# A decode attention kernel with a ring of four K/V slots in place of six, each pair finished in its own period, and wo loaded once near the end

## The chip, the cores and the metric

One NeuronCore of one Trainium2 chip runs the kernel; the other cores are idle. The metric is device microseconds (us) of one execution. Kernels are compared only within the same rounds.

Engines in the profile: PE is the matrix engine (PEld its weight loads), DVE the vector engine, ACT the scalar engine, SP the engine whose queue issues the loads.

## The reference

A block of one new token for 4 sequences: layer norm, attention over a cache, a gated feed-forward part.

```python
B, Sq, D = 4, 1, 640
Hq, Hkv, Sk, Dh, F = 32, 32, 4096, 192, 1536
q = (layernorm(x) @ wq)                      # wq: 640 x 6144
p = softmax(q k^T * Dh**-0.5)                # k_cache, v_cache: 4 x 32 x 4096 x 192, bf16
h = x + (p v) @ wo                           # wo: 6144 x 640
out = h + (silu(n @ w_gate) * (n @ w_up)) @ w_down,   n = layernorm(h)
```

K and V are 403 MB of the 424 MB that are read, and every byte is used once. There are 128 pairs of sequence and head; the kernel takes two heads at a time, so it works on 64 "pairs" of one 3.1 MB K chunk and one 3.1 MB V chunk. K62 is the K chunk of pair 62, the last but one. The chunks lie in the slots of a ring, buffers in on-chip memory that are used in turn.

## The kernel before

For pair i: DVE multiplies K by the broadcast query in two halves (`tt`), PE adds up the products with an identity matrix (`red`, 12 matmuls a half), DVE finishes the sum (`rsum`) and takes the maximum, PE and DVE carry the maximum across partitions (`max_t`, `hmax`, `max_b`), ACT forms the exponentials (`exps`), PE multiplies them with V (`pv`). Every fourth pair closes a group of two heads: `evac`, `o_t`, `o_tc`, then 12 matmuls with a piece of wo (`womm`).

The helper records all operations of an engine in program order and turns dependences into semaphores. Each engine therefore works strictly in the order in which the Python code emits.

```python
    NS, NPR = 6, 3                                   # ring slots, product buffers
    ring = [sb(f"ring{j}", [128, T, DH], BF16) for j in range(NS)]
    wosb = [sb(f"wo{j}", [128, 3, D], BF16) for j in range(2)]
    ...
    chunks = []                                      # order of the loads
    for i in range(NP - 2):
        chunks += [("K", i), ("V", i)]
    chunks += [("K", NP - 2), ("K", NP - 1), ("V", NP - 2), ("V", NP - 1)]
    ...
    def load(c):                                     # waits for the release of the chunk NS places earlier
        n = order[c]
        deps = [lambda: released[chunks[n - NS]]] if n >= NS else ([wq_used] if slot[c] >= 3 else [])
    ...
    for c in chunks:
        load(c)
        if c[0] == "V" and c[1] % B == (1 if c[1] < NP - B else B - 1):
            load_wo(c[1] // B)                       # 16 pieces; the last one behind the last V
    ...
    for i in range(NP):                              # software pipeline over three pairs
        tt(i, 0)
        if i >= 1:
            red(i - 1, 1); rsum(i - 1, 1); rmax(i - 1)
        tt(i, 1)
        ...
        if i >= 2:
            pv(i - 2)
        if i >= 1:
            max_t(i - 1); hmax(i - 1)
        red(i, 0)
        if i >= 1:
            max_b(i - 1); neg_m(i - 1); exps(i - 1)
        rsum(i, 0)
        ...
```

The feed-forward weights are loaded last, into slots of the ring that have come free.

## Time and profile before

| | before |
|---|---|
| time, median of the first 3 runs | 1001.67 us (1001.23 to 1002.71) |
| span in the profile | 1000.1 us |
| read from memory | 424.29 MB |
| load queue, share of 16 DMA engines' span | 99.2% |
| PE, DVE, ACT busy | 66%, 55%, 12% |
| mean granted PE clock | 0.831 |
| DVE waiting for K | 295.9 us |

From the page of the kernel before: the queue table (packets, MB, share of 16 engines' span), and from the slices the share of DMA (tenths) and the GB/s in 40 equal stretches of 25 us.

```profile
DMA  9999999999999999999999999999999999999996
GB/s 393 427 438 426 427 435 428 426 434 427 427 431 431 425 429 433 430 427 427 433 428 428 432 428 428 427 434 427 428 431 433 425 428 432 428 428 430 431 423 287
q1 hardware_dynamic: 21760, 424.29, 99.2%
```

The stream of loads is never interrupted: this is what bounds the kernel. The table of waits says the same from the side of compute (who waited for whom: total us, times, longest):

```profile
DVE prod L319 <- DMA ring<-in_A_k_cache_dram: 295.9, 62, 6.6
```

DVE has work for each pair only when K arrives and is idle in between. Compute is ahead of the loads.

The timeline of one pair in the middle (start, duration, engine, line, operation, count, idle time before it and who ended it):

```profile
508.83 3.36 DVE L319 TENSOR_TENSOR prod<-ring,qb 128x6144 f16<-128x6144 bf16 x1 [5.00 <-DMA ring<-in_A_k_cache_dram]
512.96 3.35 DVE L319 TENSOR_TENSOR prod<-ring,qb 128x6144 f16<-128x6144 bf16 x1
514.02 4.90 PE L97 MATMUL pb<-prod,identH 128*128 128x512 f16 x11
519.39 2.54 PE L97 MATMUL pb<-prod,identH 128*128 128x512 f16 x11
```

PE was idle before the first reduction, and its eleven matmuls took 4.90 us there; at full clock eleven take 2.54 us. The stretch-by-stretch view shows why: the granted clock was 0.50 from 512.0 to 518.5 us and 1.00 from 519.0 us.

The end of the timeline:

```profile
958.54 3.36 DVE L319 TENSOR_TENSOR prod<-ring,qb 128x6144 f16<-128x6144 bf16 x1 [4.83 <-DMA ring<-in_A_k_cache_dram]
983.89 0.83 PE L391 MATMUL pb<-ring,pbuf 128*16 128x384 bf16 x16
990.83 1.77 PE L522 MATMUL pb<-wg_sb,lnT 128*4 128x384 bf16 x20 [1.90 <-DVE lnT L266]
995.82 1.77 PE L532 MATMUL pb<-wd_sb,guT 128*4 128x160 bf16 x48 [1.62 <-DVE guT L528]
998.00 0.67 SPq L536 DMA_DIRECT2D out_dram<-outsb  x2
```

The last PV ends at 984.72 us. Then 15.4 us of serial work follow: transposes, wo, layer norm, feed-forward, output. The loads stop at about 995 us, so compute and stream end together, and neither has much to give.

### The profile page before, as it was taken

What the parts mean: (1) busy time and instruction counts of PE and PEld (TensorE: products, weight loads), DVE (VectorE), ACT (ScalarE), POOL (GpSimd) and SP (SyncE); (2) the same over time, 40 slices, a digit from 0 to 9 for tenths busy, and PEclk for the clock granted to TensorE, in tenths of its full rate; (3) what the DMA queues carried; (4) which work ended last, traced back from release to release, by engine and by line L of the source; (5) the groups of instructions that cost most, each with busy time, mean ns of one, the idle gap of its engine ahead of it and who ended that gap; (6) DMA issues with size and microseconds to landing.
All of it is one profiled execution on the core that took longest, in us unless ns stands there. A gap on an engine that the chain in (4) does not pass through costs nothing.

```text
span 1000.1 us, 9429 instructions
## 1 busy us (share of the span) xinstructions
PE 661.4 (66%) x4752; PEld 122.6 (12%) x3344; DVE 547.6 (55%) x450; ACT 122.6 (12%) x412; POOL 4.5 (0%) x19
## 2 busy tenths in 40 slices
PE   0676676676676676676677686676676666676686
PEld 0110110111110110110111110110110111110112
DVE  2546556546546546556546546546556546546562
ACT  0110111110110110111010110111011010110112
POOL 1000000000000000000000000000000000000000
PEclk9887887877887887887887877988888887987887
DMA  9999999999999999999999999999999999999996
GB/s 393 427 438 426 427 435 428 426 434 427 427 431 431 425 429 433 430 427 427 433 428 428 432 428 428 427 434 427 428 431 433 425 428 432 428 428 430 431 423 287
DMA packets 21849, 424.90 MB, mean 425 GB/s; under 512 B 2480, under 2 KB 2480, under 8 KB 4912
## 3 DMA queue, kind: packets, MB, share of 16 engines
q1 hardware_dynamic: 21760, 424.29, 99.2%
q8 instruction: 32, 0.52, 0.2%
q14 instruction: 9, 0.07, 0.0%
q10 hardware_dynamic: 48, 0.01, 0.0%
HBM read 424.29 MB, written 0.01 MB: 424 GB/s over the span
## 4 chain that ended last, share of the span: by engine, by line
DMA 65%; PE 23%; DVE 10%; SPq 1%; issue 1%; ACT 0%; ACTq 0%; DVEq 0%
DMA ring<-in_A_k_cache_dram 63%; PE pb L97 13%; DVE prod L319 8%; PE pb L391 3%; DMA xrow<-in_A_x_dram 2%; PE pb L329 2%; DVE sc L335 1%; PE pb L344 1%; PE pb L412 1%; PE pb L353 1%; SPq L304 1%; PE pb L286 1%; DVE msb L340 1%; PE pb L374 0%; PE pb L522 0%
## 5 line engine op out<-in xcount | busy, mean ns | idle before, releaser
L319 DVE TENSOR_TENSOR prod<-ring,qb 128x6144 f16<-128x6144 bf16 x128 | 429.1, 3353 | 303.6 <-DMA ring<-in_A_k_cache_dram 295.9
L97 PE MATMUL pb<-prod,identH 128*128 128x512 f16 x1408 | 434.2, 472 | 0.0
L344 PE MATMUL pb<-identF,msb 128*1 128x128 f32 x128 | 33.9, 362 | 301.7 <-DVE msb L340 301.7
L335 DVE TENSOR_REDUCE sc<-pb 128x32 f32<-128x512 f32 x128 | 88.1, 688 | 112.5 <-PE pb L97 112.5
L358 ACT ACTIVATE negM<-pb 128x2 f32<-128x2 f32 x64 | 11.0, 172 | 713.5 <-PE pb L353 713.5
L391 PE MATMUL pb<-ring,pbuf 128*16 128x384 bf16 x2048 | 94.7, 326 | 0.2 <-ACT pbuf L365 0.2
L365 ACT ACTIVATE pbuf<-sc,negM 64x64 bf16<-64x64 f32 x128 | 73.9, 577 | 3.0
L329 PE MATMUL pb<-prod,identH 128*128 128x512 f16 x128 | 61.3, 479 | 3.2 <-DVE prod L319 3.2
L353 PEld LDWEIGHTS pb<-negMc,ones_row 1*128 1x128 f32 x128 | 19.3, 189 | 280.5 <-issue 258.1
L391 PEld LDWEIGHTS pb<-ring,pbuf 128*16 128x16 bf16 x2048 | 46.4, 89 | 27.5 <-issue 0.5
L344 PEld LDWEIGHTS pb<-identF,msb 128*1 128x1 f32 x128 | 5.5, 81 | 329.0 <-DVE msb L340 329.0
L365 ACT ACTIVATION_READ_ACCUMULATOR pbuf<-sc,negM 64x1 f32 x128 | 41.8, 326 | 0.0
L380 ACT ACTIVATE qb<-pb 128x192 bf16<-128x192 f32 x64 | 21.2, 331 | 103.2 <-PE pb L374 103.2
L374 PEld LDWEIGHTS pb<-qsb,sel 4*64 4x64 bf16 x128 | 6.7, 101 | 163.2 <-issue 161.6
L353 PE MATMUL pb<-negMc,ones_row 1*128 1x2 f32 x128 | 24.8, 261 | 0.7 <-DVE negMc L348 0.7
L412 PE MATMUL pb<-r,orow 128*64 128x4 f32 x384 | 20.0, 231 | 0.6 <-ACT orow L399 0.6
L412 PEld LDWEIGHTS pb<-r,orow 128*64 128x64 f32 x384 | 18.6, 174 | 2.4 <-ACT orow L399 1.0
L374 PE MATMUL pb<-qsb,sel 4*64 4x192 bf16 x128 | 17.2, 265 | 1.0 <-ACT qsb L290 0.6
L348 DVE TENSOR_REDUCE negMc<-pb 1x2 f32<-1x128 f32 x64 | 17.4, 271 | 0.5 <-PE pb L344 0.5
L329 PEld LDWEIGHTS pb<-prod,identH 128*128 128x128 f16 x128 | 12.7, 99 | 32.7 <-issue 28.3
L256 PE MATMUL pb<-mv,quadm 128*128 128x2 f32 x4 | 1.2, 363 | 23.4 <-DVE mv L254 23.4
L340 DVE TENSOR_REDUCE msb<-sc 128x1 f32<-128x64 f32 x64 | 14.1, 220 | 2.2
(61 smaller groups left out, 76.1 us busy)
## 6 DMA issues: line engine op xcount, KB each, us to landing
ring<-in_A_k_cache_dram SPq DMA_DIRECT2D x64, 3072.0 KB, 29.8
ring<-in_A_v_cache_dram SPq DMA_DIRECT2D x63, 3072.0 KB, 22.8
wq_sb<-in_A_wq_dram SPq DMA_DIRECT2D x1, 7680.0 KB, 21.0
wo<-in_A_wo_dram SPq DMA_DIRECT2D x16, 480.0 KB, 23.5
ring<-in_A_v_cache_dram SPq DMA_DIRECT2D x2, 1536.0 KB, 19.3
wg_sb<-in_B_w_gate_dram SPq DMA_DIRECT2D x1, 1920.0 KB, 25.8
wu_sb<-in_B_w_up_dram SPq DMA_DIRECT2D x1, 1920.0 KB, 18.9
wd_sb<-in_B_w_down_dram SPq DMA_DIRECT2D x1, 960.0 KB, 20.8
```

What stands on the lines that cost most here:

```text
L97: return e.add_instruction(mybir.InstMatmult(name=e.bass.get_next_instruction_name(), engine=mybir.EngineType.PE, start_tensor_calc=start, ...
L319: tk["tt", n] = op("dve", lambda e: e.tensor_tensor(out=prod[n % NPR][:, :, :], in0=ring[slot[c]][:, h * TH:(h + 1) * TH, :], in1=qbs[i % ...
L329: tk["red", n] = op("pe", lambda e, j=j: (e.matmul if j == 0 else partial(held_matmul, e))(psR[n % 3][:, 0:TH * R], lhsT=identH[:, :], rhs ...
L335: tk["rsum", n] = op("dve", lambda e: e.tensor_reduce(sc[i % 3][:, h * TH:(h + 1) * TH], psR[n % 3][:, 0:TH * R].rearrange("q (t r) -> q t ...
L340: tk["rmax", i] = op("dve", lambda e: e.tensor_reduce(msb[i % 2][:, 0:1], sc[i % 3][:, :], AX.X, ALU.max), [g("rsum", 2 * i), g("rsum", 2 ...
L344: tk["maxT", i] = op("pe", lambda e: e.matmul(psS[0:1, 0:128], lhsT=msb[i % 2][:, 0:1], rhs=identF[:, :], start=True, stop=True), [g("rmax ...
L353: tk["maxB", i] = op("pe", lambda e: e.matmul(psS[:, 128:130], lhsT=ones_row[0:1, :], rhs=negMc[i % 2][0:1, 0:2], start=True, stop=True), ...
L365: tk["exp", i] = op("act", lambda e, hh=hh, r=r: e.activation(out=pbuf[b][r, :, 2 * b + hh], in_=sc[i % 3][r, :], func=ACTF.Exp, bias=negM ...
L374: tk["qb", i] = op("pe", lambda e, hh=hh: e.matmul(psQ[64 * hh:64 * hh + 64, 0:DH], lhsT=sel[32 * n:32 * n + B, b, :], rhs=qsb[32 * n:32 * ...
L380: tk["qbc", i] = op("act", lambda e: e.activation(out=qbs[i % 2][:, :], in_=psQ[:, 0:DH], func=ACTF.Copy, scale=QS), [g("qb", i), g("tt", ...
L391: tk["pv", i] = op("pe", lambda e, t=t, n=n: e.matmul(psO[p % 2][32 * n:32 * n + 4 * B, 0:2 * DH], lhsT=pbuf[b][:, t:t + 2, :].rearrange(" ...
L412: tk["oT", p] = op("pe", lambda e, j=j, hh=hh, k=k: e.matmul(psO[p % 2][64 * hh:64 * hh + 64, OC + B * j:OC + B * (j + 1)], lhsT=orow[p % ...
```

## The change

The intent is a simpler kernel with the same stream. The ring shrinks to four slots, which leaves room for wq in a place of its own. V1 no longer waits for the query projection, wo can lie whole in wq's place later, and each pair is finished in its own period, so one set of small buffers is enough.

```diff
-    NS, NPR = 6, 3
+    NS = 4
-    wosb = [sb(f"wo{j}", [128, 3, D], BF16) for j in range(2)]
+    wqsb = sb("wq_sb", [128, CD, H * DH], BF16)
+    wosb = nc.alloc_sbuf_tensor_at("wo_sb", [128, P, 3, D], BF16, offset=at(wqsb))
...
-        deps = [lambda: released[chunks[n - NS]]] if n >= NS else ([wq_used] if slot[c] >= 3 else [])
+        deps = [lambda: released[chunks[n - NS]]] if n >= NS else []
-        if c == ("V", NP - 1):                      # only the last V in halves
+        if c[1] == NP - 1:                          # the last K and the last V in halves
...
     for c in chunks:
+        if c == ("K", NP - 2):
+            wo_land = dma("sp", lambda e: e.dma_start(
+                wosb[:, :, :, :].rearrange("q p j n -> q p (j n)"),
+                wo[:, :].rearrange("(p q j) n -> q p (j n)", q=128, j=3)), S_wo, [wq_used])
         load(c)
-        if c[0] == "V" and c[1] % B == (1 if c[1] < NP - B else B - 1):
-            load_wo(c[1] // B)
...
     for i in range(NP):
+        p, b = i // B, i % B
+        if i == NP - 2:
+            for k in range(P - 1):
+                womm(k)
         tt(i, 0)
-        (red, rsum, max, exps of pair i-1 and pv of pair i-2 between the halves)
+        red(i, 0)
+        if i + 1 < NP:
+            q_b(i + 1)
+            q_bc(i + 1)
         tt(i, 1)
+        red(i, 1)
+        if b == 0 and p >= 1:
+            inv_l(p - 1)
+            o_tc(p - 1)
+        rsum(i, 0)
+        rsum(i, 1)
+        rmax(i)
+        max_t(i)
+        hmax(i)
+        max_b(i)
+        neg_m(i)
+        exps(i)
+        pv(i)
+        if b == B - 1:
+            evac(p)
+            l_sum(p)
+            o_t(p)
```

Cut from the diff: the query copies (16 small ones instead of 4), the selection matrix, PSUM banks and buffer counts that follow from the above, and the drain code behind the loop, which falls away.

More of the change, by code (lines that the diff above doesn't have):

```diff
@@ L126, in build_kernel @@
     J = DH // R
-    NS, NPR = 6, 3
-    OC = 2 * DH
+    NS = 4
     QS = 2.0 ** -4
@@ L143, in build_kernel @@
     ring = [sb(f"ring{j}", [128, T, DH], BF16) for j in range(NS)]
-    prod = [sb(f"prod{j}", [128, TH, DH], FP16) for j in range(NPR)]
-    wosb = [sb(f"wo{j}", [128, 3, D], BF16) for j in range(2)]
-    qsb = sb("qsb", [128, 4, 2 * DH], BF16)
+    prod = [sb(f"prod{j}", [128, TH, DH], FP16) for j in range(2)]
+    wqsb = sb("wq_sb", [128, CD, H * DH], BF16)
+    qsb = sb("qsb", [B, H * DH], BF16)
     pbuf = [sb(f"pbuf{b}", [128, T, 2 * B], BF16) for b in range(B)]
     qbs = [sb(f"qb{j}", [128, DH], BF16) for j in range(2)]
-    sel = sb("sel", [128, B, 64], BF16)
+    sel = sb("sel", [B, 2, B, 128], BF16)
     identF = sb("identF", [128, 128], FP32)
@@ L162, in build_kernel @@
     mv = sb("mv", [128, 8], FP32)
-    sc = [sb(f"sc{j}", [128, T], FP32) for j in range(3)]
+    sc = [sb(f"sc{j}", [128, T], FP32) for j in range(2)]
     msb = [sb(f"msb{j}", [128, 1], FP32) for j in range(2)]
@@ L166, in build_kernel @@
     negM = [sb(f"negM{j}", [128, 2], FP32) for j in range(2)]
-    lsb = [sb(f"lsb{j}", [128, B], FP32) for j in range(2)]
+    lsb = sb("lsb", [128, B], FP32)
     invL = sb("invL", [128, B], FP32)
-    orow = [sb(f"orow{j}", [128, 2 * DH], FP32) for j in range(2)]
-    OT = [sb(f"OT{j}", [128, 3, B], BF16) for j in range(2)]
-    sig = sb("sig", [128, FQ], FP32)
+    orow = sb("orow", [128, 2 * DH], FP32)
+    OT = sb("OT", [128, P, 3, B], BF16)
+    sig = orow
+    assert FQ == 2 * DH
     gu = sb("gu", [128, FQ], BF16)
@@ L174, in build_kernel, with at @@
     outsb = sb("outsb", [128, DQ], BF16)
-    def at(j):
-        return nc.lookup_mloc(ring[j]).addr
-    assert at(5) - at(3) == 2 * T * DH * 2
-    wqsb = nc.alloc_sbuf_tensor_at("wq_sb", [128, CD, H * DH], BF16, offset=at(3))
+    def at(t):
+        return nc.lookup_mloc(t).addr
+    assert P * 3 * D == CD * H * DH
+    wosb = nc.alloc_sbuf_tensor_at("wo_sb", [128, P, 3, D], BF16, offset=at(wqsb))
     n0 = 2 * NP
-    wgsb = nc.alloc_sbuf_tensor_at("wg_sb", [128, CD, F], BF16, offset=at(n0 % NS))
-    wusb = nc.alloc_sbuf_tensor_at("wu_sb", [128, CD, F], BF16, offset=at((n0 + 1) % NS))
-    wdsb = nc.alloc_sbuf_tensor_at("wd_sb", [128, CF, D], BF16, offset=at((n0 + 2) % NS))
+    wgsb = nc.alloc_sbuf_tensor_at("wg_sb", [128, CD, F], BF16, offset=at(ring[n0 % NS]))
+    wusb = nc.alloc_sbuf_tensor_at("wu_sb", [128, CD, F], BF16, offset=at(ring[(n0 + 1) % NS]))
+    wdsb = nc.alloc_sbuf_tensor_at("wd_sb", [128, CF, D], BF16, offset=at(ring[(n0 + 2) % NS]))
     PB = [eg.enter(nc.psum_tensor(f"pb{k}", [128, 512], FP32)) for k in range(8)]
-    psR, psS, psO, psH, psQ = PB[0:3], PB[3], PB[4:6], PB[6], PB[7]
+    psR, psS, psO, psH, psQ, psL, psT = PB[0:2], PB[2], PB[3], PB[4], PB[5], PB[6], PB[7]
     S_ring = [sem(f"s_ring{j}") for j in range(NS)]
-    S_wo = [sem(f"s_wo{j}") for j in range(2)]
-    S_x, S_out, S_half = sem("s_x"), sem("s_out"), sem("s_half")
+    S_x, S_wq, S_wo, S_out, S_halfK, S_halfV = (sem(n) for n in ("s_x", "s_wq", "s_wo", "s_out", "s_halfk", "s_halfv"))
     xd = [dma("act", lambda e, n=n: e.dma_start(xrow[32 * n:32 * n + B, :], x[:, 0, n * DQ:(n + 1) * DQ]), S_x)
           for n in range(4)]
+    wq_land = dma("sp", lambda e: e.dma_start(
+        wqsb[:, :, :].rearrange("q c n -> q (c n)"), wq[:, :].rearrange("(q c) n -> q (c n)", c=CD)), S_wq)
     chunks = []
@@ L237, in build_kernel @@
         t.deps.append(zx)
-    zp = None
-    for k in (6, 0, 1, 2, 7, 4, 5):
-        zp = op("dve", lambda e, k=k: e.memset(PB[k][:, 0:2 * DH], 0.0))
+    for ps in (psH, psO):
+        zp = op("dve", lambda e, ps=ps: e.memset(ps[:, 0:2 * DH], 0.0))
     op("dve", lambda e: e.memset(epsv[:, :], eps))
-    ksel = op("dve", lambda e: e.tensor_copy(
-        out=sel[:, :, :], in_=r32[:, 0:B][:, :, None].broadcast_to([128, B, 64])), [c1])
+    zsel = op("dve", lambda e: e.memset(sel[:, :, :, :], 0.0))
+    for hh in range(2):
+        ksel = op("dve", lambda e, hh=hh: e.tensor_copy(
+            out=sel[:, hh, :, 64 * hh:64 * hh + 64], in_=r32[0:B, 0:B][:, :, None].broadcast_to([B, B, 64])), [c1, zsel])
     kquad = op("dve", lambda e: e.tensor_scalar(
@@ L275, in build_kernel @@
                                          rhs=xrow[:, :], start=True, stop=False), [kidb, zp] + xd)
-    wq_land = dma("sp", lambda e: e.dma_start(
-        wqsb[:, :, :].rearrange("q c n -> q (c n)"), wq[:, :].rearrange("(q c) n -> q (c n)", c=CD)), S_ring[3])
-    bank = [PB[0], PB[1], PB[2], PB[7]]
+    bank = [PB[0], PB[1], psQ, psL]
     qcopy = []
@@ L288, in build_kernel @@
                     rhs=wqsb[:, c, p * 2 * DH:(p + 1) * 2 * DH], start=(c == 0), stop=(c == CD - 1)),
-                    [ln1, wq_land, zp])
-        qcopy.append(op("act", lambda e, k=k: e.activation(
-            out=qsb[:, k, :], in_=bank[k][:, 0:2 * DH], func=ACTF.Copy, scale=1.0), [a]))
+                    [ln1, wq_land])
+        for n in range(4):
+            p = 4 * k + n
+            o, i_ = qsb[:, p * 2 * DH:(p + 1) * 2 * DH], bank[k][32 * n:32 * n + B, 0:2 * DH]
+            if n % 2 == 0:
+                qcopy.append(op("act", lambda e, o=o, i_=i_: e.activation(out=o, in_=i_, func=ACTF.Copy, scale=1.0), [a]))
+            else:
+                qcopy.append(op("dve", lambda e, o=o, i_=i_: e.tensor_copy(out=o, in_=i_), [a]))
     wq_used = a
+    q_done = qcopy[-2:]
     def load(c):
         n = order[c]
-        deps = [lambda: released[chunks[n - NS]]] if n >= NS else ([wq_used] if slot[c] >= 3 else [])
+        deps = [lambda: released[chunks[n - NS]]] if n >= NS else []
         r = ring[slot[c]]
-        if c == ("V", NP - 1):
+        if c[1] == NP - 1:
             s = src(c).rearrange("q (t d) -> q t d", d=DH)
-            landed[c] = [dma("sp", lambda e, a=a, k=k: e.dma_start(r[:, a:a + TH, :], s[:, a:a + TH, :]), k, deps)
-                         for a, k in ((0, S_ring[slot[c]]), (TH, S_half))]
+            landed[c] = [dma("sp", lambda e, a=a: e.dma_start(r[:, a:a + TH, :], s[:, a:a + TH, :]), k, deps)
+                         for a, k in ((0, S_ring[slot[c]]), (TH, S_halfK if c[0] == "K" else S_halfV))]
         else:
@@ L305, in load, with half @@
                              S_ring[slot[c]], deps)]
-    wo_land = {}
-    def load_wo(p):
-        wo_land[p] = dma("sp", lambda e: e.dma_start(
-            wosb[p % 2][:, :, :].rearrange("q j n -> q (j n)"),
-            wo[p * 2 * DH:(p + 1) * 2 * DH, :].rearrange("(q j) n -> q (j n)", j=3)),
-            S_wo[p % 2], [lambda: tk["womm", p - 2]] if p >= 2 else [])
+    def half(c, h):
+        return landed[c][min(h, len(landed[c]) - 1)]
     def tt(i, h):
@@ L319, in tt @@
         tk["tt", n] = op("dve", lambda e: e.tensor_tensor(
-            out=prod[n % NPR][:, :, :], in0=ring[slot[c]][:, h * TH:(h + 1) * TH, :],
+            out=prod[h][:, :, :], in0=ring[slot[c]][:, h * TH:(h + 1) * TH, :],
             in1=qbs[i % 2][:, None, :].broadcast_to([128, TH, DH]), op=ALU.mult),
-            landed[c] + [g("qbc", i), g("red", n - NPR)])
+            [half(c, h), g("qbc", i), g("red", n - 2)])
         if h == 1:
@@ L329, in red @@
             tk["red", n] = op("pe", lambda e, j=j: (e.matmul if j == 0 else partial(held_matmul, e))(
-                psR[n % 3][:, 0:TH * R], lhsT=identH[:, :], rhs=prod[n % NPR][:, :, j * R:(j + 1) * R],
-                start=(j == 0), stop=(j == J - 1)), [g("tt", n), g("rsum", n - 3), kidh, qcopy[-1]])
+                psR[h][:, 0:TH * R], lhsT=identH[:, :], rhs=prod[h][:, :, j * R:(j + 1) * R],
+                start=(j == 0), stop=(j == J - 1)), [g("tt", n), g("rsum", n - 2), kidh] + q_done)
     def rsum(i, h):
@@ L335, in rsum @@
         tk["rsum", n] = op("dve", lambda e: e.tensor_reduce(
-            sc[i % 3][:, h * TH:(h + 1) * TH], psR[n % 3][:, 0:TH * R].rearrange("q (t r) -> q t r", r=R),
-            AX.X, ALU.add), [g("red", n), g("exp", i - 3)])
+            sc[i % 2][:, h * TH:(h + 1) * TH], psR[h][:, 0:TH * R].rearrange("q (t r) -> q t r", r=R),
+            AX.X, ALU.add), [g("red", n), g("exp", i - 2)])
     def rmax(i):
-        tk["rmax", i] = op("dve", lambda e: e.tensor_reduce(msb[i % 2][:, 0:1], sc[i % 3][:, :], AX.X, ALU.max),
+        tk["rmax", i] = op("dve", lambda e: e.tensor_reduce(msb[i % 2][:, 0:1], sc[i % 2][:, :], AX.X, ALU.max),
                            [g("rsum", 2 * i), g("rsum", 2 * i + 1), g("maxT", i - 2)])
@@ L365, in exps @@
             tk["exp", i] = op("act", lambda e, hh=hh, r=r: e.activation(
-                out=pbuf[b][r, :, 2 * b + hh], in_=sc[i % 3][r, :], func=ACTF.Exp, bias=negM[i % 2][r, hh:hh + 1],
-                scale=alpha, accum_out=lsb[p % 2][r, b:b + 1]),
-                [g("negM", i), g("rsum", 2 * i + 1), g("pv", i - B), g("lsum", p - 2), pool_done])
+                out=pbuf[b][r, :, 2 * b + hh], in_=sc[i % 2][r, :], func=ACTF.Exp, bias=negM[i % 2][r, hh:hh + 1],
+                scale=alpha, accum_out=lsb[r, b:b + 1]),
+                [g("negM", i), g("rsum", 2 * i + 1), g("pv", i - B), g("lsum", p - 1), pool_done])
     def q_b(i):
         p, b = i // B, i % B
-        k, n = p // 4, p % 4
         for hh in range(2):
             tk["qb", i] = op("pe", lambda e, hh=hh: e.matmul(
-                psQ[64 * hh:64 * hh + 64, 0:DH], lhsT=sel[32 * n:32 * n + B, b, :],
-                rhs=qsb[32 * n:32 * n + B, k, hh * DH:(hh + 1) * DH], start=True, stop=True),
-                [qcopy[k], qcopy[-1], ksel, g("qbc", i - 1), tk.get("invL")])
+                psQ[:, 0:DH], lhsT=sel[:, hh, b, :], rhs=qsb[:, (2 * p + hh) * DH:(2 * p + hh + 1) * DH],
+                start=(hh == 0), stop=(hh == 1)), q_done + [ksel, g("qbc", i - 1)])
     def q_bc(i):
@@ L381, in q_bc, with pv @@
                                                         scale=QS), [g("qb", i), g("tt", 2 * (i - 2) + 1)])
-    def pv(i, lo=0, hi=T):
+    def pv(i):
         p, b = i // B, i % B
@@ L387, in pv, with l_sum @@
         v = ring[slot[c]]
-        for t in range(lo, hi, 2):
+        for t in range(0, T, 2):
             n = (t // 2) % 4
-            land = landed[c][min(t // TH, len(landed[c]) - 1)]
             tk["pv", i] = op("pe", lambda e, t=t, n=n: e.matmul(
-                psO[p % 2][32 * n:32 * n + 4 * B, 0:2 * DH],
+                psO[32 * n:32 * n + 4 * B, 0:2 * DH],
                 lhsT=pbuf[b][:, t:t + 2, :].rearrange("q t m -> q (t m)"),
                 rhs=v[:, t:t + 2, :].rearrange("q t d -> q (t d)"),
-                start=(b == 0 and t < 8), stop=(b == B - 1 and t >= T - 8)), [land, g("exp", i), g("otc", p - 2)])
+                start=(b == 0 and t < 8), stop=(b == B - 1 and t >= T - 8)),
+                [half(c, t // TH), g("exp", i), g("evac", p - 1), zp])
         released[c] = tk["pv", i]
     def evac(p):
-        tk["evac", p] = op("act", lambda e: e.activation(out=orow[p % 2][:, :], in_=psO[p % 2][:, 0:2 * DH],
-                                                         func=ACTF.Copy), [g("pv", B * p + B - 1), g("oT", p - 2)])
-    def l_sum(p, qbc_i):
-        tk["lsum", p] = op("pe", lambda e: e.matmul(psQ[:, 256:256 + B], lhsT=halfm[:, :], rhs=lsb[p % 2][:, :],
+        tk["evac", p] = op("act", lambda e: e.activation(out=orow[:, :], in_=psO[:, 0:2 * DH], func=ACTF.Copy),
+                           [g("pv", B * p + B - 1), g("oT", p - 1)])
+    def l_sum(p):
+        tk["lsum", p] = op("pe", lambda e: e.matmul(psL[:, 0:B], lhsT=halfm[:, :], rhs=lsb[:, :],
                                                     start=True, stop=True),
-                           [g("exp", B * p + B - 1), g("qbc", qbc_i), pool_done])
+                           [g("exp", B * p + B - 1), g("invL", p - 1), pool_done] + q_done)
     def o_t(p):
@@ L412, in o_t @@
                     tk["oT", p] = op("pe", lambda e, j=j, hh=hh, k=k: e.matmul(
-                        psO[p % 2][64 * hh:64 * hh + 64, OC + B * j:OC + B * (j + 1)],
-                        lhsT=orow[p % 2][:, k * DH + j:(k + 1) * DH:3],
+                        psT[64 * hh:64 * hh + 64, B * j:B * (j + 1)],
+                        lhsT=orow[:, k * DH + j:(k + 1) * DH:3],
                         rhs=r32[:, 2 * B * k + hh:2 * B * (k + 1):2], start=(k == 0), stop=(k == 1)),
-                        [g("evac", p), pool_done])
+                        [g("evac", p), g("otc", p - 1), pool_done])
     def inv_l(p):
-        tk["invL", p] = tk["invL"] = op("dve", lambda e: e.reciprocal(invL[:, :], psQ[:, 256:256 + B]), [g("lsum", p)])
+        tk["invL", p] = op("dve", lambda e: e.reciprocal(invL[:, :], psL[:, 0:B]), [g("lsum", p)])
     def o_tc(p):
         tk["otc", p] = op("dve", lambda e: e.tensor_tensor(
-            out=OT[p % 2][:, :, :], in0=psO[p % 2][:, OC:OC + 3 * B].rearrange("q (j b) -> q j b", b=B),
+            out=OT[:, p, :, :], in0=psT[:, 0:3 * B].rearrange("q (j b) -> q j b", b=B),
             in1=invL[:, None, :].broadcast_to([128, 3, B]), op=ALU.mult),
-            [g("oT", p), g("invL", p), g("womm", p - 2)])
+            [g("oT", p), g("invL", p)])
     def womm(p):
@@ L430, in womm @@
                 tk["womm", p] = op("pe", lambda e, j=j, n=n: e.matmul(
-                    psH[32 * n:32 * n + B, 0:DQ], lhsT=OT[p % 2][:, j, :],
-                    rhs=wosb[p % 2][:, j, n * DQ:(n + 1) * DQ], start=False, stop=(p == P - 1 and j == 2)),
-                    [g("otc", p), wo_land[p]])
+                    psH[32 * n:32 * n + B, 0:DQ], lhsT=OT[:, p, j, :],
+                    rhs=wosb[:, p, j, n * DQ:(n + 1) * DQ], start=False, stop=(p == P - 1 and j == 2)),
+                    [g("otc", p), wo_land])
     for c in chunks:
+        if c == ("K", NP - 2):
+            wo_land = dma("sp", lambda e: e.dma_start(
+                wosb[:, :, :, :].rearrange("q p j n -> q p (j n)"),
+                wo[:, :].rearrange("(p q j) n -> q p (j n)", q=128, j=3)), S_wo, [wq_used])
         load(c)
-        if c[0] == "V" and c[1] % B == (1 if c[1] < NP - B else B - 1):
-            load_wo(c[1] // B)
     q_b(0)
@@ L442, in build_kernel @@
     for i in range(NP):
+        p, b = i // B, i % B
+        if i == NP - 2:
+            for k in range(P - 1):
+                womm(k)
         tt(i, 0)
-        if i >= 1:
-            red(i - 1, 1)
-            rsum(i - 1, 1)
-            rmax(i - 1)
-        tt(i, 1)
+        red(i, 0)
         if i + 1 < NP:
@@ L451, in build_kernel @@
             q_bc(i + 1)
-        if i >= 4 and (i - 4) % B == 3:
-            womm((i - 4) // B)
-        if i >= 3 and (i - 3) % B == 3:
-            p = (i - 3) // B
-            o_t(p)
-            l_sum(p, i + 1 if i + 1 < NP else i)
-        if i >= 2:
-            pv(i - 2)
-            if (i - 2) % B == 3:
-                evac((i - 2) // B)
-        if i >= 1:
-            max_t(i - 1)
-            hmax(i - 1)
-        red(i, 0)
-        if i >= 1:
-            max_b(i - 1)
-            neg_m(i - 1)
-            exps(i - 1)
-        rsum(i, 0)
-        if i >= 3 and (i - 3) % B == 3:
-            p = (i - 3) // B
-            inv_l(p)
-            o_tc(p)
-    i = NP - 1
-    red(i, 1)
-    rsum(i, 1)
-    rmax(i)
-    max_t(i)
-    hmax(i)
-    max_b(i)
-    neg_m(i)
-    exps(i)
-    load_act = op("act", lambda e: e.activation(out=mv[:, 3:4], in_=epsv[:, 0:1], func=ACTF.Sqrt))
-    if ("womm", P - 2) not in tk:
-        womm(P - 2)
-    pv(i - 1)
-    pv(i, 0, TH)
-    l_sum(P - 1, i)
+        tt(i, 1)
+        red(i, 1)
[14 more added lines that the diff above has]
+            l_sum(p)
+            o_t(p)
+    op("act", lambda e: e.activation(out=stats[:, 7:8], in_=epsv[:, 0:1], func=ACTF.Sqrt))
     inv_l(P - 1)
-    pv(i, TH, T)
-    evac(P - 1)
-    o_t(P - 1)
     o_tc(P - 1)
@@ L513, in build_kernel @@
             wd_land[c] = t
-    zg = op("dve", lambda e: e.memset(PB[0][:, 0:FQ], 0.0), [g("red", 2 * NP - 1)])
+    zg = op("dve", lambda e: e.memset(PB[0][:, 0:FQ], 0.0))
     zg = op("dve", lambda e: e.memset(PB[1][:, 0:FQ], 0.0))
```

## The prediction

> **What bounds the kernel now.** The DMA engines. The queue table says the loading queue's packets fill 99.2% of 16 engines' span, and the slices show 423 to 438 GB/s from the second slice to the last but one. 424.29 MB are read[...].  In the table of waits DVE waits 295.9 us for K to land: compute is ahead of the loads. In the timeline the last weights land at about 995.5 us (issued at 973, 22 us to landing), so one K/V pair costs the stream (estimate: 994 us x 6.29/424.29 MB) 14.7 us. The end is nearly balanced: the last PV ends at 984.7 and 15.4 us of serial work follow to 1000.1.
>
> **What the change does.** Bytes are the same: wo moves from 16 pieces to one, 7.9 MB, in front of the last two pairs. The start is the same: wq, K0, V0, K1 are issued at once in both; V1, issued at 31.2 us before, was not needed earlier. No saving on the bound.
>
> The software pipeline goes: pair i's PV now stands in front of pair i+1's reduction on PE. Costs from the timeline (us): tt 3.35 each; twelve-matmul reduction 2.75 at full clock, 5.2 at half; from the end of the second reduction to the negated maximum 1.7; from there to the end of the exponentials 1.9; PV 1.5 at full clock (about 2.6 at half, estimate). Serial period, when K is already there: 1.9+1.5 to 2.6 (tt(i+1,0) hides under it), both reductions 6.4 to 7.7 with a mixed clock, query broadcast 0.3, 1.7: 12.5 to 14. Every fourth period adds evacuation and transposes, about 1.9, so 0.5 on average: 13 to 14.5, below 14.7. Still DMA-bound, barely.
>
> With 4 slots: K lands at 0, its slot is free at 6.8, V's slot at about 17, and the stream needs V's successor issued by 29. At least 12 us of loads stay queued. Time to landing: about 20 to 22 us.
>
> **Clock.** Before, it falls to 0.50 some 2 to 4.5 us after PE goes idle and returns 5 to 6 us into the next work[...]. After, I expect a mean of 0.75 to 0.9.
>
> **Tail.** K62 lands near 960, V63 near 982. PV(62) now precedes pair 63's reductions: PV(62) ends at 976.5 to 977.5, the second reduction of 63 at 983 to 984.5, the last PV at 988 to 991 against 984.7 before. The unchanged 15.4 us follow. So 3.4 to 6.2 us longer. K63 in halves gains nothing: DVE is busy with pair 62 until after K63 has landed. The 15 early wo matmul groups (6 to 8 us) fit between wo's landing and K62's.
>
> **Prediction.** 1006 us, 8 in 10 between 1001 and 1014. Chances: faster by over 2%: 0.01; within 2%: 0.90; slower by over 2%: 0.09.
>
> **To check.** DMA share stays at 99%, GB/s per slice 423 to 438 (right), or falls to about 400 with DVE no longer waiting for K (compute-bound: wrong). DVE's wait for K falls from 296 us to below 150. Last PV ends 3 to 6 us later while the last wd lands at the same 995.
>
> **What would make it wrong.** A serial period above 14.7 us (both reductions at half clock: about 16.5); a queue that runs dry; the one large wo load running below the stream's rate.

The sum came to 1006 us, the time of before and 3.4 to 6.2 us of tail.

## The result, and the profile after

| | before | after |
|---|---|---|
| time, median of 4 runs each | 1002.02 us (1001.23 to 1002.71) | 1004.62 us (1004.4 to 1007.1) |
| ratio | | 1.0032, 95% interval 1.0014 to 1.005 |
| span in the profile | 1000.1 us | 1005.3 us (the slowest of the 4 runs) |
| load queue, share | 99.2% | 98.8% |
| PE, DVE busy | 66%, 55% | 69%, 56% |
| mean granted PE clock | 0.831 | 0.801 |
| DVE waiting for K | 295.9 us | 156.9 us |
| K, V issue to landing | 29.8, 22.8 us | 22.5, 19.5 us |

Ratios are the mean time of one kernel's fast runs over that of the other's fast runs of the same rounds, so they are not quite the ratio of the medians quoted. By the 2% measure the two are the same; the interval says that the change costs a little.

The same lines of the page and of the waits, after:

```profile
DMA  9999999999999999999999999999999999999994
GB/s 392 433 434 426 432 425 433 427 433 428 430 432 429 431 426 433 425 434 426 433 428 431 429 428 431 429 431 429 430 431 431 429 428 432 427 431 424 417 421 205
q1 hardware_dynamic: 21664, 424.29, 98.8%
DVE prod L320 <- DMA ring<-in_A_k_cache_dram: 156.9, 58, 22.7
```

The stream is as dense as before through 900 us. DVE still waits for K, though for half as long: the loop is still bound by the loads. The last slice is emptier (205 against 287 GB/s), because a longer end without loads lies in it.

One pair in the middle:

```profile
514.10 6.63 DVE L320 TENSOR_TENSOR prod<-ring,qb 128x6144 f16<-128x6144 bf16 x2 [0.19 <-DMA ring<-in_A_k_cache_dram]
515.90 2.74 PE L389 MATMUL pb<-ring,pbuf 128*16 128x384 bf16 x32 [1.56 <-ACT pbuf L366]
518.68 0.33 SPq L310 DMA_DIRECT2D ring<-in_A_v_cache_dram  x1
518.98 2.59 PE L97 MATMUL pb<-prod,identH 128*128 128x512 f16 x11
528.71 6.63 DVE L320 TENSOR_TENSOR prod<-ring,qb 128x6144 f16<-128x6144 bf16 x2 [2.44 <-DMA ring<-in_A_k_cache_dram]
```

PV of the pair before stands in front of the first reduction. It came after a thin stretch of PE (1.24 us of work in the 4 us from 511.7) and took 2.74 us, at a granted clock of 0.50 from 515.7 to 519.1 us, against 1.48 us at full clock in before. The next V is issued as soon as that PV has ended. The next K is taken up 14.6 us later, after a wait of 2.44 us, which is what this one period has to spare (the periods of a group of four differ; on average it is about 1 us, see n2).

The end:

```profile
918.33 20.76 SPq L310 DMA_DIRECT2D ring<-in_A_k_cache_dram  x1
952.83 4.78 PE L429 MATMUL pb<-wo_sb,OT 128*4 128x160 bf16 x180 [10.65 <-DMA wo_sb<-in_A_wo_dram]
960.12 6.63 DVE L320 TENSOR_TENSOR prod<-ring,qb 128x6144 f16<-128x6144 bf16 x2 [22.65 <-DMA ring<-in_A_k_cache_dram]
974.82 2.74 PE L389 MATMUL pb<-ring,pbuf 128*16 128x384 bf16 x32 [2.08 <-DMA ring<-in_A_v_cache_dram]
981.47 2.54 PE L97 MATMUL pb<-prod,identH 128*128 128x512 f16 x11
987.73 2.74 PE L389 MATMUL pb<-ring,pbuf 128*16 128x384 bf16 x32 [1.55 <-ACT pbuf L366]
996.79 1.77 PE L500 MATMUL pb<-wg_sb,lnT 128*4 128x384 bf16 x20 [1.90 <-DVE lnT L268]
1003.18 0.67 SPq L514 DMA_DIRECT2D out_dram<-outsb  x2
```

The products of pair 62 begin at 960.12 us, against 958.54 us before. PV of pair 62 waits for its V and holds PE until 977.56; only then do the reductions of pair 63 run, to 984.01. The last PV ends at 990.47 us instead of 984.72. The loads end where they did: the DMA share from 995 to 996 us is 0.07, in before 0.01.

### The profile page after: what moved, and what is told of

Read it like the earlier page. It is cut to its first block, busy times and chain, and to the rows that moved or that the text cites. A ratio compares the mean times of both kernels' runs of the same rounds, so it can differ in the third digit from the quotient of the medians.

```text
span 1005.3 us, 9377 instructions
## 1 busy us (share of the span) xinstructions
PE 692.3 (69%) x4752; PEld 146.0 (15%) x3344; DVE 560.3 (56%) x455; ACT 123.9 (12%) x416; POOL 4.7 (0%) x19
## 3 DMA queue, kind: packets, MB, share of 16 engines
q1 hardware_dynamic: 21664, 424.29, 98.8%
HBM read 424.29 MB, written 0.01 MB: 422 GB/s over the span
## 4 chain that ended last, share of the span: by engine, by line
DMA 68%; DVE 21%; PE 8%; ACT 1%; issue 1%; SPq 0%; ACTq 0%; DVEq 0%
DMA ring<-in_A_k_cache_dram 63%; DVE prod L320 19%; PE pb L97 4%; DMA ring<-in_A_v_cache_dram 3%; DMA xrow<-in_A_x_dram 2%; PE pb L389 2%; ACT pbuf L366 1%; PE pb L330 1%; DVE sc L336 0%; PE pb L500 0%; DVE qsb L296 0%; PE pb L286 0%; PE pb L411 0%; PE pb L345 0%; PE pb L354 0%
## 5 line engine op out<-in xcount | busy, mean ns | idle before, releaser
L320 DVE TENSOR_TENSOR prod<-ring,qb 128x6144 f16<-128x6144 bf16 x128 | 424.0, 3354 | 157.9 <-DMA ring<-in_A_k_cache_dram 156.9
L97 PE MATMUL pb<-prod,identH 128*128 128x512 f16 x1408 | 388.6, 433 | 0.0
L389 PE MATMUL pb<-ring,pbuf 128*16 128x384 bf16 x2048 | 161.3, 487 | 101.4 <-ACT pbuf L366 99.3
L330 PE MATMUL pb<-prod,identH 128*128 128x512 f16 x128 | 59.0, 461 | 75.5 <-DVE prod L320 75.4
L389 PEld LDWEIGHTS pb<-ring,pbuf 128*16 128x16 bf16 x2048 | 65.0, 117 | 159.8 <-issue 149.5
L345 PE MATMUL pb<-identF,msb 128*1 128x128 f32 x128 | 24.3, 271 | 66.4 <-DVE msb L341 66.4
L374 PEld LDWEIGHTS pb<-qsb,sel 4*128 4x128 bf16 x128 | 7.1, 93 | 235.6 <-issue 233.3
L374 PE MATMUL pb<-qsb,sel 4*128 4x192 bf16 x128 | 22.2, 255 | 2.0 <-DVE qsb L296 2.0
## 6 DMA issues: line engine op xcount, KB each, us to landing
ring<-in_A_k_cache_dram SPq DMA_DIRECT2D x63, 3072.0 KB, 22.5
ring<-in_A_v_cache_dram SPq DMA_DIRECT2D x63, 3072.0 KB, 19.5
```

What stands on the lines that cost most here:

```text
L97: return e.add_instruction(mybir.InstMatmult(name=e.bass.get_next_instruction_name(), engine=mybir.EngineType.PE, start_tensor_calc=start, ...
L320: tk["tt", n] = op("dve", lambda e: e.tensor_tensor(out=prod[h][:, :, :], in0=ring[slot[c]][:, h * TH:(h + 1) * TH, :], in1=qbs[i % 2][:, ...
L330: tk["red", n] = op("pe", lambda e, j=j: (e.matmul if j == 0 else partial(held_matmul, e))(psR[h][:, 0:TH * R], lhsT=identH[:, :], rhs=pro ...
L345: tk["maxT", i] = op("pe", lambda e: e.matmul(psS[0:1, 0:128], lhsT=msb[i % 2][:, 0:1], rhs=identF[:, :], start=True, stop=True), [g("rmax ...
L374: tk["qb", i] = op("pe", lambda e, hh=hh: e.matmul(psQ[:, 0:DH], lhsT=sel[:, hh, b, :], rhs=qsb[:, (2 * p + hh) * DH:(2 * p + hh + 1) * DH ...
L389: tk["pv", i] = op("pe", lambda e, t=t, n=n: e.matmul(psO[32 * n:32 * n + 4 * B, 0:2 * DH], lhsT=pbuf[b][:, t:t + 2, :].rearrange("q t m - ...
```

## The experiments

Theory A: the loop is still bound by the same stream, and all the loss lies in the end game, where nothing overlaps any longer. Rival B: the stream itself has lost time, through the shallower ring or through the one large load of wo. Rival C: the loop is already bound by its serial compute and only happens to be near the stream's time.

The first four kernels ran in the same rounds, with nine runs of before (median 1001.32 us).

### The changed kernel again (a0_after), no edit

> The changed kernel again, unaltered, in the same rounds as the others. Both theories: 1004.5 us (1003.8 to 1005.5), ratio to before 1.0025 to 1.0035. The profile seen so far was of the slowest of four runs (span 1005.3 against 1002.6 in two others); I want to see whether the extra 2.7 us of that one lies in the stream or in the tail.

Measured: 1006.27 us (1004.85 to 1006.88), ratio 1.0045 (1.0033 to 1.0058). The median is 0.8 us above the range that I expected, and the ratio above it too, though its interval overlaps that of the first rounds. The executions of this kernel spread over 2 us. The profiled execution (span 1004.6 us) had its products of pair 62 at 960.20, like the first, so the stream is repeatable; its last PV took 1.48 us and ended at 989.17, earlier than in the first profile, while pair 63's products began at 973.53, later than in the first (972.23). So these two executions differ in the tail and not in the stream.

### The last two pairs pipelined (e1_tail)

```diff
+        if i == NP - 2:                 # i is 62, z is 63
+            tt(i, 0); red(i, 0); q_b(z); q_bc(z); tt(i, 1); red(i, 1)
+            tt(z, 0)
+            rsum(i, 0); rsum(i, 1); rmax(i); max_t(i); hmax(i)
+            tt(z, 1); red(z, 0)
+            max_b(i); neg_m(i); exps(i)
+            red(z, 1)
+            pv(i)
+            rsum(z, 0); rsum(z, 1); rmax(z); max_t(z); hmax(z); max_b(z); neg_m(z); exps(z)
+            pv(z); evac(p); l_sum(p); o_t(p)
+            break
```

> Only the order of the last two pairs is altered: pair 63's products and first reduction are put in front of pair 62's softmax, and PV(62) behind both reductions of 63, as the kernel before does. Theory A (the loss is the serial tail alone): the last PV ends at about 985 us and the time falls by 2 to 4 us against the changed kernel, to 1000.5 to 1002.5, the same as before within 0.1%. Rival B (the stream itself lost time, through the shallower ring or the one large wo load): no more than 0.5 us is regained, since the last weights still land late; the time stays at 1004 or above.

Measured: 1003.81 us (1003.16 to 1005.82), ratio 1.0025 (1.0013 to 1.0038); 2.46 us less than the changed kernel of the same rounds by the medians, 2.0 us by the means (1004.05 and 1006.05); the two intervals against before just overlap. Its timeline at the end:

```profile
959.90 6.63 DVE L320 TENSOR_TENSOR prod<-ring,qb 128x6144 f16<-128x6144 bf16 x2 [22.69 <-DMA ring<-in_A_k_cache_dram]
968.23 3.36 DVE L320 TENSOR_TENSOR prod<-ring,qb 128x6144 f16<-128x6144 bf16 x1 [1.70 <-ACT qb L379]
984.70 1.48 PE L389 MATMUL pb<-ring,pbuf 128*16 128x384 bf16 x32 [1.55 <-ACT pbuf L366]
```

The last PV ends at 986.18. The order of the tail is therefore about half of the loss. The time did not come down to the expected 1000.5 to 1002.5 us: pair 62 still starts 1.4 us later than in before. In before one piece of wo, 0.5 MB, stands behind the last V; here all of wo stands in front of the last two pairs.

### The last K whole again (e2_k63_whole)

```diff
-        if c[1] == NP - 1:
+        if c == ("V", NP - 1):
```

> The last K is loaded in one piece again. Theory A: DVE takes up pair 63 some 5 us after K63 has landed, so nothing changes: within 0.5 us of the changed kernel. Rival (the halves let pair 63 start earlier): 1 to 3.7 us slower than the changed kernel (3.7 us is half of a K landing).

Measured: 1006.8 us (1004.7 to 1007.71), 0.5 us above the changed kernel, the intervals overlap (1.0033 to 1.006 against 1.0033 to 1.0058). In its timeline DVE takes up pair 63 at 972.33 us without any wait for K. The halves of K do nothing, as predicted.

### wo in pieces (e3_wo_pieces)

```diff
-        if c == ("K", NP - 2):
-            wo_land = (one load of all of wo)
         load(c)
+        if c[0] == "V" and c[1] % B == 1 and c[1] < NP - 2:
+            k = c[1] // B
+            wo_land = dma("sp", ... wosb[:, k] <- wo[k * 2 * DH:(k + 1) * 2 * DH] ..., S_wo, [wq_used])
```

> wo is loaded in 16 pieces, one per four pairs, into the same place; its matmuls stay near the end. Theory A: the bytes are the same and the stream is the bound, so within 1 us of the changed kernel; the 20.8 us that the queue spent on issuing the K behind the large wo load goes away, and the GB/s of the slices 37 to 39 return to about 428, worth at most 1 us. Rival B (the large wo load costs the stream): 2 us or more faster than the changed kernel.

Measured: 1005.82 us (1003.91 to 1007.94), ratio 1.0044 (1.0031 to 1.0056): 0.45 us less than the changed kernel, inside the noise. Slices 37 to 39 went from 424, 417, 421 GB/s (first profile of the changed kernel) to 429, 430, 421, and issuing the K behind it took 0.33 us instead of 20.76 us. That the queue was held for 20.8 us behind the large load cost no more than this: in the first profile of the changed kernel the DMA share in these 20.8 us was 0.99, at 411 GB/s. What held the issue is not shown: behind wq, as many bytes (7.9 MB) in rows of 61440 bytes against 3840 in wo, the next issue took 0.42 us, but there the queue was still empty. Rival B in its second form falls.

The next four kernels ran in other rounds, with seven runs of before (median 1001.53 us).

### Compute without the stream: before (n1_before_noload) and after (n2_after_noload)

The same edit in both; the results are wrong, since every later pair uses what lies in its slot. (The comparison with the reference passed all the same, presumably because the attention part of the output is too small for its tolerance; this was not tested.)

```diff
         n = order[c]
+        if n >= NS:
+            landed[c] = landed[chunks[n % NS]]
+            return
```

> Wrong on purpose: only the first six K/V chunks are loaded, every later pair computes on what is in its slot. It measures the compute period of the kernel before without the stream. From the trace: DVE 8.6 us and PE about 8.5 us of work per pair and few waits, so a period of 9 to 10.5 us and 620 to 720 us in all. If the loop of before were not bound by the stream, the time would stay near 1000.

> Wrong on purpose: only the first four K/V chunks are loaded. It measures the serial period of the changed kernel. My theory (serial period just below the stream's 14.7 us): the trace shows 13.64 us between products at the start, where K was already there, and every fourth pair 1.9 us more, so about 14.1 us, 930 to 955 us in all. Rival (the loop is already bound by compute, the full stream a coincidence): 985 us or more. If the serial period were far below, as a warm PE would make it (12 us), 840 us or less.

Measured: 614.77 us for before (614.07 to 615.46), 923.54 us for the changed kernel (923.13 to 923.94). The timeline of DVE in the changed kernel without loads; the starts tell the period. The last two lines are from before without loads, two starts four pairs apart:

```profile
520.16 6.61 DVE L323 TENSOR_TENSOR prod<-ring,qb 128x6144 f16<-128x6144 bf16 x2
536.50 6.61 DVE L323 TENSOR_TENSOR prod<-ring,qb 128x6144 f16<-128x6144 bf16 x2
548.78 6.61 DVE L323 TENSOR_TENSOR prod<-ring,qb 128x6144 f16<-128x6144 bf16 x2
561.19 6.61 DVE L323 TENSOR_TENSOR prod<-ring,qb 128x6144 f16<-128x6144 bf16 x2
574.77 6.61 DVE L323 TENSOR_TENSOR prod<-ring,qb 128x6144 f16<-128x6144 bf16 x2
308.65 3.35 DVE L322 TENSOR_TENSOR prod<-ring,qb 128x6144 f16<-128x6144 bf16 x1
342.73 3.35 DVE L322 TENSOR_TENSOR prod<-ring,qb 128x6144 f16<-128x6144 bf16 x1
```

Periods of 16.3, 12.3, 12.4 and 13.6 us: 54.61 us for four pairs, 13.65 us for one. Before, four pairs took 34.08 us in the like kernel (308.65 to 342.73 us), 8.52 us for one. The stream needs about 14.7 us (estimate of the prediction). So the change made the compute of the loop 60% longer, from far below the stream to 7% below it, and none of it shows in the time. Rival C falls. The total is a little lower than I expected (930 to 955 us), the period lies in the predicted 13 to 14.5 us.

### The pipelined kernel with four slots (n3_before_4slots)

```diff
-    NS, NPR = 6, 3
+    NS, NPR = 4, 3
-    wqsb at the place of ring slots 3 to 5
+    wqsb at the place of the product buffers, with a rest behind them
-        deps = ... if n >= NS else ([wq_used] if slot[c] >= 3 else [])
+        deps = ... if n >= NS else []
```

> The kernel before, pipelined as it is, but with 4 ring slots (wq gets a place of its own over the product buffers). Theory: the pipelined order frees V(i) only about 29.7 us after K(i) has landed, and the stream needs it by 29.4, less the issue: the queue runs dry for some us in every pair, 1050 to 1100 us. So finishing a pair in its own period is what makes 4 slots enough. Rival (slots are plentiful, 4 suffice in either order): 1002 us within 0.5%.

Measured: 1101.24 us (1090.23 to 1102.74), ratio 1.0971 (1.0917 to 1.1026), at the upper edge of what I expected. Its page and its waits:

```profile
q1 hardware_dynamic: 21760, 424.29, 93.0%
DVE prod L323 <- DMA ring<-in_A_k_cache_dram: 386.0, 61, 9.2
```

and the load and PV lines of one period in its timeline:

```profile
506.12 1.48 PE L395 MATMUL pb<-ring,pbuf 128*16 128x384 bf16 x32
507.64 0.33 SPq L308 DMA_DIRECT2D ring<-in_A_v_cache_dram  x1
508.67 0.43 SPq L308 DMA_DIRECT2D ring<-in_A_k_cache_dram  x1
```

V is issued the moment PV has freed its slot, and the stream is nearly empty by then: 217 GB/s from 506 to 508 us, 184 GB/s from 508 to 510. In the pipelined order PV of a pair runs one period later, and its V stays in the ring as long. So the two parts of the change belong together: four slots alone would have cost 10%; finishing a pair in its own period is what makes them enough.

### The changed kernel with three slots (n4_after_3slots)

```diff
-    NS = 4
+    NS = 3
+    spare = sb("spare", [128, T, DH], BF16)      # the down weights go here, without a wait
```

> The changed kernel with 3 ring slots; the down weights get the space of the fourth, so the tail is not held up. Theory: V(i)'s slot is free 17 us after K(i)'s landing and its successor is needed at 22 us[...]: 3 us of margin, so at most 1% slower than the changed kernel, 1004 to 1014 us, with time to landing falling to 10 to 16 us. Rival (the ring of 4 has no margin): the queue runs dry in each pair and the time rises by 5% or more.

The count came to 3 us of margin with a term that no trace had shown; it is cut, so 22 less 17 us do not give them.

Measured: 1027.59 us (1023.66 to 1031.33), ratio 1.0259 (1.0223 to 1.0295). It is neither the at most 1% of my count nor the 5% of the rival. K landed 12.9 us after its issue, V 15.4 us. In one place of the timeline the next K was issued 11.4 us after the V ahead of it, some 4 us before that V landed (estimate from the 15.4 us):

```profile
502.35 0.33 SPq L311 DMA_DIRECT2D ring<-in_A_v_cache_dram  x1
513.71 0.33 SPq L311 DMA_DIRECT2D ring<-in_A_k_cache_dram  x1
526.82 6.63 DVE L321 TENSOR_TENSOR prod<-ring,qb 128x6144 f16<-128x6144 bf16 x2 [2.29 <-DMA ring<-in_A_k_cache_dram]
```

Yet the stream fell to 262, 295 and 319 GB/s in the three us from 515 to 518. My margin was counted to the landing, and by that estimate the stream thinned out before it; why is not shown. What is shown: a fourth slot is worth 2.1 to 2.3% here (1027.59 against 1004.62 to 1006.77 us), and the ring of four has no such dips in the stretch looked at (385 GB/s or more in every us from 500 to 530). The term from my count was an assumption; in n3 about 2.4 us passed from the issue of V at 507.64 to the return of the stream, 406 GB/s from 510 to 512.

The last four kernels ran in a third set of rounds, with nine runs of before (median 1001.52 us).

### The changed kernel once more (a1_after), no edit

> The changed kernel once more, as the yardstick of these rounds. 1004 to 1007 us, 0.3 to 0.5% above before; the spread between executions (2 to 3 us, against 1.5 us of before) stays.

Measured: 1006.77 us (1005.03 to 1006.84), ratio 1.0051 (1.0037 to 1.0064). The profile is of the fastest execution, span 1003.2 us: pair 62 begins at 960.12, exactly as in the first profile, and the last PV takes 1.50 us and ends at 988.42. Again the stream is the same and the tail differs.

### Pipelined tail and the last piece of wo behind the last V (e5_tail_wo)

```diff
 (the tail of e1_tail, and)
         load(c)
+        if c[0] == "V" and c[1] % B == (1 if c[1] < NP - B else B - 1):
+            k = c[1] // B
+            wo_land[k] = dma("sp", ... piece k ..., S_wo if k < P - 1 else S_wo15, [wq_used])
```

> The pipelined last two pairs, and besides them wo in 16 pieces with the last piece behind the last V, as in before; ring of 4 and own-period loop stay. The pipelined tail alone left K62 landing at 959.9 us against 958.5 in before, and its last PV 1.5 us later. Theory A (all the loss is in the end game: tail order, and 0.5 MB of wo standing in front of the last pairs instead of behind them): K62 lands at about 958.6 us, the last PV ends at 984.5 to 985.5, the time equals before within 0.1%, 1000.7 to 1002.3 us. Rival (some of the loss is spread over the loop by the ring of 4): it stays 2 us or more above before.

Measured: 1003.37 us (1002.03 to 1004.05), ratio 1.0015 (1.0003 to 1.0028), 3.4 us below the changed kernel. The profiled execution, the fastest of five, did what theory A says: span 1000.1 us, as before; and at the end

```profile
958.69 6.63 DVE L320 TENSOR_TENSOR prod<-ring,qb 128x6144 f16<-128x6144 bf16 x2 [3.43 <-DMA ring<-in_A_k_cache_dram]
983.63 1.66 PE L389 MATMUL pb<-ring,pbuf 128*16 128x384 bf16 x32 [1.55 <-ACT pbuf L366]
```

K62 comes at 958.69 (958.54 in before), the last PV ends at 985.29. But the median stays 1.85 us above before, outside my range. Nothing in the one profile accounts for it. The executions spread over 2.0 us, and I take it for tail timing, but e5 alone does not show this; the next but one does more.

### Keeping PE busy in the last pair (e6_warm_tail)

```diff
+    def fill(n):                       # matmuls into a free bank, never read
+        for _ in range(n):
+            op("pe", lambda e: e.matmul(psQ[:, 0:TH * R], lhsT=identH[:, :], rhs=prod[0][:, :, 0:R], start=True, stop=True), ...)
         red(i, 1)
+        if i == NP - 1: fill(4)
         exps(i)
+        if i == NP - 1: fill(6)
         pv(i)
```

> The changed kernel with ten matmuls of no use in the two gaps of the last pair (4 behind its last reduction, 6 in front of its PV), into a free bank; the result is unaltered. In the changed kernel the last PV took 2.74 us at a clock falling to 0.50, against 1.48 us at full clock. Theory (the cold clock is about 1.3 us of the loss): the last PV takes 1.5 to 1.8 us, the time falls by 1 to 1.5 us against the changed kernel. Rival (the clock falls on its own schedule, or the fillers cost what they gain): no change within 0.5 us.

Measured: 1006.15 us (1005.45 to 1006.43), ratio 1.0044 (1.0032 to 1.0057), 0.6 us below the changed kernel with overlapping intervals. In the profile the clock stays at 1.00 through 990 us and the last PV takes 1.48 us. But in two of the three profiles of the changed kernel the last PV takes 1.5 us without any filler, and in that of a0 the clock stays at 1.00 to 992 us; so it is not shown that the fillers kept it up. So the cold PV of the first profile is a part of the spread, not of the median loss. The expected 1 to 1.5 us were not found.

### wo behind the last V (e7_wo_last)

```diff
-        if c == ("K", NP - 2):
-            wo_land = (one load of all of wo)
         load(c)
+    for h in range(4):                 # four quarters, a semaphore each, behind all K and V
+        t = dma("sp", ... wosb[:, 4 * h:4 * h + 4] <- wo[...] ..., sem(f"s_wo{h}"), [wq_used])
...
-        if i == NP - 2:
-            for k in range(P - 1):
-                womm(k)
...
-    womm(P - 1)
+    for k in range(P):
+        womm(k)
```

> wo, which the change allows to lie whole in wq's place, is loaded behind the last V, in four quarters, instead of in front of the last two pairs; all its matmuls follow the last attention output. Theory: the last V lands about 18 us earlier (near 964), the serial tail of pair 63 runs under the load of wo and the feed-forward weights, and the kernel ends some 4 us behind the last landing at 995.3: 999 to 1001 us, faster than the changed kernel by 4 to 6 us and than before by 0 to 2 us. Rival (the end is set by compute behind the last weights, not by where V63 stands): no gain against the changed kernel.

Measured: 1000.88 us (1000.63 to 1000.94), ratio 0.9992 (0.998 to 1.0005). This is 5.9 us below the changed kernel and level with before (the interval includes 1; the medians differ by 0.6 us). The order of the loop and of its serial last pairs is that of the changed kernel; only wo and its matmuls have moved. The end of its timeline:

```profile
940.51 6.63 DVE L320 TENSOR_TENSOR prod<-ring,qb 128x6144 f16<-128x6144 bf16 x2 [2.71 <-DMA ring<-in_A_k_cache_dram]
966.99 1.69 PE L389 MATMUL pb<-ring,pbuf 128*16 128x384 bf16 x32 [1.56 <-ACT pbuf L366]
981.86 1.77 PE L429 MATMUL pb<-wo_sb,OT 128*4 128x160 bf16 x48 [3.05 <-DMA wo_sb<-in_A_wo_dram]
991.04 1.77 PE L502 MATMUL pb<-wu_sb,lnT 128*4 128x384 bf16 x20 [2.24 <-DMA wu_sb<-in_B_w_up_dram]
996.60 0.67 SPq L516 DMA_DIRECT2D out_dram<-outsb  x2
```

Pair 62 starts 20 us earlier, the last PV ends at 968.68, and from there PE waits for weights, not weights for PE. With the tail hidden under loads, the executions agree within 0.3 us, against 1.8 us for the changed kernel and 2.25 us for before. Both say that loss and spread of the changed kernel sat in its exposed tail. And since this loop, on four slots and in its serial order, delivers the last weights in time for 1000.88 us (the loads end as in before: DMA share 0.09 from 995 to 996 us and 0.01 after), the loop itself has lost nothing: rival B falls in its first form too.

## Why the prediction was right or wrong

The prediction was 1006 us (1001 to 1014); measured were 1004.62 us at first, 1006.27 and 1006.77 us in later rounds. Its mechanism held. Against before, 4 us more were predicted; the medians differ by 2.6 us in the first rounds, less than the 3.4 to 6.2 us foreseen for the tail, and by 4.95 and 5.25 us later, so that the nearness of 1006 to the measured time is in part luck.

- **The bound is the stream, and the change leaves it alone.** Right: 424.29 MB in both, share 99.2 and 98.8%, a mean of 424 and 422 GB/s over the span, the loads end in the same us, and e7 shows that the loop costs nothing.
- **A serial period of 13 to 14.5 us, just under 14.7.** Right: 13.65 us measured by itself (n2). The mixed clock that I assumed is in the trace: PV 2.74 us in the middle of the loop, reductions of 2.54 to 4.90 us for eleven matmuls from 500 to 620 us, a mean of 0.801 (predicted 0.75 to 0.9). What makes the clock fall is not shown: before the PV at 515.90 us, PE had gaps of at most 1.6 us, and the clock fell at 515.7 us. In the tail of the first profile PE worked 1.04 us of the 4 us from 984 to 988, with no gap over 1.6 us, and the clock went from 1.00 to 0.50; in a0 it worked 1.06 us of the same 4 us and the clock stayed at 1.00. In before, from 500 to 620 us, the clock fell 2.1 to 5.2 us after PE went idle and returned 3.0 to 6.1 us into the next work, a wider range than I wrote.
- **Four slots suffice.** Right: K lands 22.5 us after its issue and V 19.5 us, predicted 20 to 22. They suffice only in the new order (n3: 10% slower in the old one). My way of counting the margin is too generous, as three slots show (n4).
- **The tail is 3.4 to 6.2 us longer.** Right: the last PV ended 5.75 us later in the first profile, 4.45 and 3.7 us in the two others (989.17 and 988.42 against 984.72). PV of pair 62 ended at 977.56 (predicted 976.5 to 977.5), the second reduction of 63 at 984.01 (983 to 984.5). Reordering it gave back 2.5 us, and also putting one piece of wo behind V63 3.4 us in all; 1.85 us between that kernel and before are not located to an instruction. The "unchanged" 15.4 us behind the last PV were 14.8, 15.4 and 14.8 us in the three profiles.
- **The last K in halves gains nothing.** Right (e2).
- **Sizes that were off.** The 15 groups of wo took 4.78 us and not 6 to 8. DVE's wait for K fell to 156.9 us, not below 150; 22.7 us of it is the one wait during the load of wo, which I had not subtracted. Slices 38 and 39 fell to 417 and 421 GB/s, just outside my band; loading wo in pieces (e3) brought the first back to 430 and was worth no more than noise. None of these changed the sum.

## What to carry to other kernels

In a kernel bound by its loads, compute in the loop may grow up to the stream's period for nothing (here from 8.52 to 13.65 us a pair, with about 14.7 us for the stream by the estimate); what costs is the compute that stands behind the last load, so look at the last pair, not at the loop. When a simplification frees the order of loads, use that freedom for the end: put in front what has the longest chain behind it, and load last what is used last with little work (here wo and the feed-forward weights), which was worth more than pipelining the tail (5.9 us against 2.5 us). The number of buffers and the order of work must be judged together, and a margin in the queue should not be counted to the landing of a load: three slots, counted that way, had 3 us to spare by my count and cost over 2%.
